# Seven products for the last two chunks in both layers, weight sums made in layer one's first half, token sums one step after the turned tile

## The chip, the cores and the metric

The kernel runs on one core of one Trainium2 chip. The time is the device time of one execution in microseconds (us), and what is compared is the median over several runs. Beside it there is one execution taken by the hardware profiler; its rows and spans are in us, with the mean of one instruction in ns. The engines are called as in the profile: PE (TensorE, the matrix products) with PEld (its weight loads), DVE (VectorE), ACT (ScalarE), POOL (GpSimd) and SP (SyncE, which mostly issues transfers, DMAs).

## The reference

The input x has 2048 tokens of 512 features. Four residual blocks follow each other: a linear attention, a gated mixer, and the same two again with the same weights. Everything is fp32.

```python
def _A_ref(x, wqkv, wo):                  # linear attention, 32 heads of 16
    q, k, v = ...                         # x @ wqkv, split by head
    phi = lambda t: jnp.where(t > 0, t + 1, jnp.exp(t)) + 1e-6
    pq, pk = phi(q), phi(k)
    kv = jnp.einsum("bhsd,bhse->bhde", pk, v)
    z = jnp.einsum("bhsd->bhd", pk)
    num = jnp.einsum("bhqd,bhde->bhqe", pq, kv)
    den = jnp.einsum("bhqd,bhd->bhq", pq, z)[..., None] + 1e-6
    return merged(num / den) @ wo

def _B_ref(x, w_in, w_sp, b_sp, w_out):   # w_in 512x1792, w_sp 2048x2048, w_out 896x512
    z = _gelu(jnp.einsum("bsd,df->bsf", x, w_in))
    z1 = z[..., :Fh]                      # Fh = 896
    z2 = _layernorm(z[..., Fh:], axis=-1)
    g = jnp.einsum("ts,bsf->btf", w_sp, z2) + b_sp[None, :, None]
    return jnp.einsum("bsf,fd->bsd", z1 * g, w_out)

x = x + _A_ref(_layernorm(x), A_wqkv, A_wo)
x = x + _B_ref(_layernorm(x), B_w_in, B_w_sp, B_b_sp, B_w_out)
x = x + _A_ref(_layernorm(x), A_wqkv, A_wo)
x = x + _B_ref(_layernorm(x), B_w_in, B_w_sp, B_b_sp, B_w_out)
```

## The kernel before

**Numbers.** Every fp32 operand is split into a high part, which ACT writes (`high`, L101), and a low part, the operand minus the high part, which DVE (`low`, L104) or POOL (L109) writes. A product of two operands is three products on PE into the same bank of PSUM: high by high, high by low, low by high (`mm3`, L115 to L117). PE is the engine that all others serve.

**Tiles and memory.** The 2048 tokens are 16 tiles of 128 rows; four tiles make a chunk of 512 tokens. Buffers come from pools that are written out by hand: `pages` (128x512, 22 of them, "pg" in the profile), `quads` (four times that, "qd"), `bigs` ("bg") and `banks` (the eight banks of PSUM). An instruction that takes a buffer waits until its last reader is done. Each engine executes its own instructions in the order of the program, so the order in the code is the order of the queues. A step issues work for several tiles at once: tile s at the start of the pipeline, tile s-1, s-2 and so on further down.

**A layer** (L = 0, "layer one", and L = 1, "layer two", the same code) is an attention and a mixer:

- *P1*, steps 1 to 17, the first half of the attention: normalise a tile (`ln_a`, `ln_b`), turn it (by PE against `ident` or by a trip through DRAM, L286), split it, project to keys and queries, sum the keys (on POOL, L372), and add the tile's product with its keys into four banks `G` (`Gmm`). For the very first tile `start` lets PE run idle products (L434) while operands are on their way.
- *transition*: the sum of the keys is scaled (L505), split with its low part on POOL, and multiplied by ones (L515, L516); `G` is split and multiplied down to the matrix `W2`. In between stand the score scalings of the first tiles (`a`, on POOL, L590; `a2_den` and `a2_mul`, on DVE).
- *P2*, steps 1 to 18: `b` splits a scaled query tile, `c` multiplies it by `W2`, `c2` adds the residual (L643), `c_stats` and `c3` normalise it and send it through DRAM to be turned, `d_high` and `d_low` (one step later) split the turned tile into its chunk's pair of quads `xT`, `e` makes the z2 half of the mixer's first product (448 columns at a time), `f` the z1 half (seven blocks of 128 features by four chunks, 12 products each). From step 8 on `sums.tick` makes sums of blocks of `w_sp` on POOL (L978), which both layers' *P4* need; in layer one P2 does so besides its own work.
- a tail of z1 products, then *P4*: the product with `w_sp`, made of seven products of half-size blocks in place of eight (L1103 to L1105), the gates (POOL, L1123 and L1125), and the product with `w_out` tile by tile (`o`, addition L1198, store L1200). While layer one's `o` runs, `join` begins the next layer's P1.

**Seven products for the last two chunks.** In layer two alone (`self.seven`), the z1 blocks 0 to 5 of the chunks 2 and 3 are not made by `f`. The features are paired (block g with block g + 3) and so are the chunks, and the 2x2 block product is made in seven products P1 to P7 in place of eight. This needs sums of blocks of the weight and sums of blocks of tokens. The weight sums are made in layer one's `o` loop by the class `Make` (load, four additions on DVE, split, store into the DRAM tile `kept`), and fetched in layer two's P2 by `fetch_sum` (POOL's queue). The token sums are made by DVE as each turned tile of chunk 3 arrives (`block_sums`, inside `d_low`), from that tile and the tile of chunk 2 that POOL has put together again (`whole`); `block_parts` splits them.

```python
            if s == 16:                       # part of side(), layer two's P2
                self.P2(1)
                self.P2(2)
                self.fetch_sum(2)
                for m in (2, 3):
                    self.block_parts(m, 0)
```

In layer one the same blocks are 12 products each of `f`, in the steps and in a loop ahead of P4.

Of the kernel before, what the change touches and what calls it, by code (L numbers as in the profile page):

```python
# [53 lines left out]
def mixer_kernel(ctx: ExitStack, tc: tile.TileContext, x_in, wqkv, wo_d, win1_d, win2_d, wsp_d, bsp_d, wout_d,  # L54
# [109 lines left out]

    class Make:


        def __init__(self):
            self.raw, self.sum, self.part = {}, {}, {}

        def fetch(self, g):
            self.raw[g] = load(win1_d[g]), load(win1_d[g + 3])

        def add(self, g):
            a, b = self.raw.pop(g)
            A11, A12, A21, A22 = (r.rearrange("p (c f) -> p c f", f=P)[:, s] for r in (a, b) for s in (slice(0, 2), slice(2, 4)))
            s, t = pages.get([P, 2, 2, P]), pages.get([P, 2, 2, P])
# [4 lines left out]
            pages.put(a, b)  # L182
            self.sum[g] = s, t

        def split(self, g):
            self.part[g] = []
            for r in self.sum.pop(g):
                h, l = pages.get([P, 2, 2, P], F32R), pages.get([P, 2, 2, P], F32R)
                split(h, l, r)
                pages.put(r)  # L190
                self.part[g] += [h, l]

        def store(self, g):
            for n, p in enumerate(self.part.pop(g)):
                m = 2 * (n // 2)
                nc.sync.dma_start(kept[:, m:m + 2, g, n % 2, :], p.bitcast(F32).rearrange("p m c f -> p m (c f)"))
                pages.put(p)

        def step(self, i):
            for g in range(3):  # L200
                at = i - 2 * g
                if 0 <= at < 5:
                    (self.fetch, lambda g: None, self.add, self.split, self.store)[at](g)
# [87 lines left out]
    class P1:  # L291
# [124 lines left out]
        def start(self):  # L416
# [19 lines left out]
            idle(10)  # L436
# [3 lines left out]
            self.wk.piece()  # L440
            self.T_high(0)
            idle(4)
# [3 lines left out]
            self.wk.piece()  # L446
# [9 lines left out]
        def run(self):  # L456
# [5 lines left out]
            for s in range(1, NT + 2):  # L462
# [34 lines left out]
                for w in list(side)[:1 if s < 5 else 2]:  # L497
                    w.fetch()

# [69 lines left out]
    class P2:  # L569
        def __init__(self, p1):  # L570
# [7 lines left out]
            self.seven = self.L == 1  # L578
            self.S, self.T, self.Tp = {}, {}, {}
# [92 lines left out]
        def d_low(self, i):  # L672
# [40 lines left out]
        def f(self):  # L713
# [8 lines left out]
            if f == NF - 1 and not (self.seven and n == 3):  # L722
                quads.put(*self.xT.pop(n))
# [15 lines left out]
        def whole(self, k):  # L739

            h, l = (t[:, :, k * P:(k + 1) * P].bitcast(F32) for t in self.xT[2])
            self.xr = pages.get([P, 4, P])
            nc.gpsimd.tensor_tensor(self.xr, h, l, op=OP.add)

        def block_sums(self, k, y):


            p, o = divmod(k, 2)
# [4 lines left out]
            x = self.xr  # L753
# [5 lines left out]
            pages.put(x)  # L759
# [42 lines left out]
        def P1(self, g):  # L802
            if g == 0:
                self.X, self.C = [], []
            self.X.append(banks.get(PAGE))
            self.product(self.X[g], "P1", g, start=True)
            self.C.append(self.copied(self.X[g]))

        def P2(self, g):
            y = banks.get(PAGE)  # L810
            self.product(y, "P2", g, start=True, stop=True)
            t = self.C[g]
# [4 lines left out]
        def last_f(self, n):  # L817
            self.fq.append((n, NF - 1))
            self.f()

        def tail(self, p4):
            self.last_f(3)
# [38 lines left out]
        def side(self, s):  # L861

            if s == 14:
                self.P1(0)
                self.P1(1)
            elif s == 15:
                self.P1(2)
                self.P2(0)
                self.fetch_sum(4)
            elif s == 16:  # L870
                self.P2(1)
                self.P2(2)
# [12 lines left out]
            if 13 <= s < 17:  # L885
                self.whole(s - 13)

        def run(self, sums):
            w1 = self.win1
            for s in range(1, NT + 3):  # L890
# [16 lines left out]
                else:  # L907
# [32 lines left out]
                if self.seven:  # L940
                    self.side(s)
# [59 lines left out]
    class P4:  # L1001
# [189 lines left out]
        def o(self, i):  # L1191
# [6 lines left out]
            nc.vector.tensor_add(x, x, b)  # L1198
            banks.put(b)
            nc.sync.dma_start(xs[2 * self.L + 2, i], x)  # L1200
# [117 lines left out]
```

## Time and profile before

| | before |
|---|---|
| median of 3 runs | 1393.01 us (1392.59 to 1393.34) |
| profiled execution: its own time | 1392.76 us |
| its span (first to last instruction) | 1391.0 us |
| granted clock of PE | 1.0 |
| PE busy | 1383.0 us, 99% of the span |
| DVE busy | 908.8 us, 65% |
| ACT busy | 595.1 us, 43% |
| POOL busy | 429.2 us, 31% |
| DMA traffic | 233.57 MB, mean 168 GB/s |

A row of the timeline or of a group gives the start (timeline only), the busy time, the engine, the line of the code, the operation, what it writes and reads, and the shapes. A bracket at the end of a timeline row is the idle time of that engine just before the instruction and what ended it. A row of a group ends with the number of instructions, their busy time, the mean of one in ns, and the idle time before them with what ended most of it. In the list of waits the three numbers are the sum, the count and the longest wait.

### The profile page before, as it was taken

How to read it: one execution, taken by the hardware profiler on the slowest of the kernel's cores; microseconds unless marked ns; L12 is line 12 of the kernel's file. 1: busy time of each engine (PE TensorE's matmuls, PEld its weight loads, DVE VectorE, ACT ScalarE, POOL GpSimd, SP SyncE). 2: the span in 40 equal slices, each digit the busy share in tenths (PEclk: the TensorE clock that was granted, in tenths of full speed). 3: DMA queues.
4: the chain of work that ended last, by engine and by line, in shares of the span. 5: the costliest groups of instructions: out<-in, count | busy, mean ns of one | idle time of the engine just before them, and what ended most of it. 6: DMA issues, size and time to landing. Idle time of an engine off the chain costs nothing.

```text
span 1391.0 us, 17707 instructions
## 1 busy us (share of the span) xinstructions
PE 1383.0 (99%) x6252; PEld 1159.9 (83%) x6252; DVE 908.8 (65%) x1305; ACT 595.1 (43%) x922; POOL 429.2 (31%) x518
## 2 busy tenths in 40 slices
PE   9999999999999999999999999999999999999998
PEld 7888888888888888888888888888878888888887
DVE  6785777853755587666667767876666345776642
ACT  6674543444442234241366755444454432342410
POOL 3343344544135541431023424432320001123310
PEclk9999999999999999999999999999999999999999
DMA  5541256766678864357745313555454323434442
GB/s 174 171 132 59 91 167 224 260 228 211 212 246 287 297 228 137 122 203 241 266 130 177 112 45 122 174 175 173 124 187 152 106 91 129 174 129 159 167 145 90
DMA packets 148313, 233.57 MB, mean 168 GB/s; under 512 B 12416, under 2 KB 54144, under 8 KB 148224
## 3 DMA queue, kind: packets, MB, share of 16 engines
q1 hardware_dynamic: 144768, 226.15, 49.0%
q0 software_dynamic: 1728, 3.15, 0.8%
q10 hardware_dynamic: 1728, 3.15, 0.6%
q8 instruction: 49, 0.80, 0.2%
q14 instruction: 40, 0.33, 0.1%
HBM read 161.35 MB, written 71.04 MB: 167 GB/s over the span
## 4 chain that ended last, share of the span: by engine, by line
PE 96%; DVE 2%; ACT 1%; POOL 1%; issue 1%; ACTq 0%; POOLq 0%
PE bank L117 18%; PE bank L116 18%; PE bank L115 18%; PE bank L1105 13%; PE bank L1104 13%; PE bank L1103 13%; PE bank L247 1%; PE bank L793 0%; PE bank L792 0%; PE bank L791 0%; DVE st L222 0%; PE bank L434 0%; ACT qd L101 0%; ACT pg L235 0%; DVE pg L286 0%
## 5 line engine op out<-in xcount | busy, mean ns | idle before, releaser
L1104 PE MATMUL bank<-qd,pg 128*128 128x512 f32 x800 | 311.2, 389 | 0.0
L1105 PE MATMUL bank<-qd,pg 128*128 128x512 f32 x800 | 311.2, 389 | 0.0
L1103 PE MATMUL bank<-qd,pg 128*128 128x512 f32 x800 | 311.2, 389 | 0.0
L1069 DVE TENSOR_TENSOR qd<-qd,qd 128x1024 fp32r<-128x1024 f32 x112 | 158.4, 1414 | 138.7 <-ACT qd L1062 138.5
L1062 ACT ACTIVATE qd<-qd 128x1024 fp32r<-128x1024 f32 x112 | 118.6, 1059 | 235.9 <-DMA qd<-s 96.5
L1125 POOL TENSOR_TENSOR bg<-bg,pg 128x512 f32<-128x512 f32 x56 | 78.2, 1399 | 327.6 <-DMA pg<-z 302.9
L1104 PEld LDWEIGHTS bank<-qd,pg 128*128 128x128 f32 x800 | 150.2, 188 | 31.4
L1103 PEld LDWEIGHTS bank<-qd,pg 128*128 128x128 f32 x800 | 150.2, 188 | 31.3
L1105 PEld LDWEIGHTS bank<-qd,pg 128*128 128x128 f32 x800 | 150.2, 188 | 30.8
L117 PE MATMUL bank<-qd,pg 128*128 128x512 f32 x384 | 149.9, 390 | 0.0
L226 POOL TENSOR_SCALAR rs<-mv 128x1 f32<-128x1 f32 x96 | 38.5, 401 | 333.5 <-DVE mv L224 320.3
L978 POOL TENSOR_TENSOR pg<-pg,pg 128x512 f32<-128x512 f32 x64 | 93.7, 1464 | 93.8 <-DMA pg<-in_wsp_dram 85.4
L235 ACT ACTIVATE pg<-pg,nb,rs 128x512 f32<-128x512 f32 x63 | 51.1, 811 | 161.8 <-POOL nb L229 155.6
L115 PE MATMUL bank<-qd,pg 128*128 128x512 f32 x288 | 112.3, 390 | 0.0
L116 PE MATMUL bank<-qd,pg 128*128 128x512 f32 x288 | 112.2, 390 | 0.0
L115 PE MATMUL bank<-bg,qd 128*128 128x448 f32 x256 | 94.2, 368 | 1.6 <-ACT qd L101 1.6
L117 PE MATMUL bank<-bg,qd 128*128 128x448 f32 x256 | 93.6, 366 | 0.1
L116 PE MATMUL bank<-bg,qd 128*128 128x448 f32 x256 | 93.6, 366 | 0.0
L101 ACT ACTIVATE pg<-pg 128x512 fp32r<-128x512 f32 (+1 forms) x83 | 51.0, 616 | 96.5 <-DVE pg L286 51.9
L115 PE MATMUL bank<-wo,qd 128*128 128x512 f32 x224 | 87.1, 389 | 0.0
L116 PE MATMUL bank<-wo,qd 128*128 128x512 f32 x224 | 87.1, 389 | 0.0
L117 PE MATMUL bank<-wo,qd 128*128 128x512 f32 x224 | 87.1, 389 | 0.0
(156 smaller groups left out, 2689.7 us busy)
## 6 DMA issues: line engine op xcount, KB each, us to landing
qd<-s SPq DMA_DIRECT2D x64, 512.0 KB, 3.4
qd<-in_wsp_dram SPq DMA_DIRECT2D x48, 512.0 KB, 4.2
pg<-in_wsp_dram SPq DMA_DIRECT2D x64, 256.0 KB, 5.0
s<-pg SPq DMA_DIRECT2D x64, 256.0 KB, 4.8
pg<-x SPq DMA_DIRECT2D x64, 256.0 KB, 3.3
pg<-z SPq DMA_DIRECT2D x56, 256.0 KB, 3.7
x<-pg SPq DMA_DIRECT2D x48, 256.0 KB, 2.6
z<-pg SPq DMA_DIRECT2D x44, 256.0 KB, 2.9
```

Source lines behind the costliest of these rows:

```text
L101: nc.scalar.activation(h, src, AF.Copy)
L115: nc.tensor.matmul(out, ah, bh, start=start, stop=False)
L116: nc.tensor.matmul(out, ah, bl, start=False, stop=False)
L117: nc.tensor.matmul(out, al, bh, start=False, stop=stop)
L235: nc.scalar.activation(y, x, AF.Identity, bias=nb, scale=rs)
L978: nc.gpsimd.tensor_tensor(t, a, b, op=OP.add)
L1062: nc.scalar.activation(w[:, 0], r, AF.Copy)
L1069: nc.vector.tensor_sub(w[:, 1], r, w[:, 0].bitcast(F32))
L1103: m(out, h[:, o], w[:, 0, j, :], start=start, stop=False, skip_group_check=True)
L1104: m(out, h[:, o], w[:, 1, j, :], start=False, stop=False, skip_group_check=True)
L1105: m(out, l[:, o], w[:, 0, j, :], start=False, stop=stop, skip_group_check=True)
L1125: nc.gpsimd.tensor_tensor(u, u, z1, op=OP.mult)
```

## The change

- The switch `self.seven` goes: both layers take the seven products for chunks 2 and 3, and both end P2 with `tail`.
- `Make` runs once, in layer one's P1 (steps 15 to 17) and P2 (steps 1 to 7), by the table `PLAN`: "f0" loads block pair 0, "a0" makes its four sums, "s0" splits one of the two result pages, and every step first stores what the step before split. The four sums are now made in place and on POOL, one depending on another; the order in `kept` follows (`FORMS`).
- The token sums stand one step later. `d_low` of chunk 3 keeps the turned tile in `held`, and `block_sums` (from step 15 on) takes it a step later, behind the next tile's `d_low`. It adds up the tile of chunk 2 on DVE, in place of `whole` on POOL. The splits `block_parts` move to the steps 17 (two of them) and 18 (six), the fetches of the weight sums to 16, 17 and 18; the forms P1 and P2 are spread over the steps 14 to 17.
- In the start, ten idle products become eight and four become two; the second piece of the key weight is split ahead of the first tile, in place of behind its high part.
- One more load for the sums of `w_sp` is issued at step 7 of P2; `nxt.T(1)` (split of the next layer's second tile) moves ahead of the last `o` of layer one; the last output tile of layer two is added and stored in two halves, the second half's store on ACT's queue.

The diff, cut to its core:

```diff
...
+    FORMS = (2, 4, 3, 1)
     class Make:
         def add(self, g):
-            nc.vector.tensor_add(s[:, 0], A21, A22)
-            nc.vector.tensor_sub(s[:, 1], s[:, 0], A11)
-            nc.vector.tensor_sub(t[:, 0], A11, A21)
-            nc.vector.tensor_sub(t[:, 1], A12, s[:, 1])
+            A11, A12, A21, A22 = (r[:, s] for r in self.raw[g] for s in (slice(0, 256), slice(256, 512)))
+            G = nc.gpsimd.tensor_tensor
+            G(A22, A21, A22, op=OP.add)
+            G(A21, A11, A21, op=OP.subtract)
+            G(A11, A22, A11, op=OP.subtract)
+            G(A12, A12, A11, op=OP.subtract)
         def split(self, g):
...
+            r = self.raw[g].pop(0)
+            h, l = pages.get(PAGE, F32R), pages.get(PAGE, F32R)
+            split(h, l, r)
+            pages.put(r)
+            self.part.append((g, 2 - 2 * len(self.raw[g]), h, l))
+        def store(self):
+            for g, m, *parts in self.part:
+                for n, p in enumerate(parts):
+                    nc.sync.dma_start(kept[:, m:m + 2, g, n, :], p.bitcast(F32).rearrange("p (m f) -> p m f", m=2))
+                    pages.put(p)
+            self.part = []
+        PLAN = {("P1", 15): ("f0",), ("P1", 16): ("a0", "f1"), ("P1", 17): ("s0", "a1"), ("P2", 1): ("s0",),
+                ("P2", 2): ("s1",), ("P2", 3): ("s1", "f2"), ("P2", 5): ("a2",), ("P2", 6): ("s2",), ("P2", 7): ("s2",)}
+        def step(self, at):
+            self.store()
+            for what in self.PLAN.get(at, ()):
+                {"f": self.fetch, "a": self.add, "s": self.split}[what[0]](int(what[1]))
...
-            idle(10)
+            idle(8)
             self.ln_a(0)
             self.ln_a(1)
             self.ln_b(0)
             self.wk.piece()
+            self.wk.piece()
             self.T_high(0)
-            idle(4)
+            idle(2)
             banks.put(b)
             pages.put(m, f)
             self.T_low(0)
-            self.wk.piece()
             self.ln_b(1)
             self.wk.piece()
             self.wk.piece()
...
                     side.popleft().piece()
                 for w in list(side)[:1 if s < 5 else 2]:
                     w.fetch()
+                if self.L == 0:
+                    make.step(("P1", s))
         def d_low(self, i):
             b, home, h, l = self.dpart
             low(l, b, h)
             n, k = divmod(i, 4)
-            if self.seven and n == 3:
-                self.block_sums(k, b)
-            home.put(b)
+            if n == 3:
+                self.held.append((k, b))
+            else:
+                home.put(b)
             if i in self.xB:
                 pages.put(self.xB.pop(i))
-            if k == 3 and not (self.seven and n >= 2):
+            if k == 3 and n < 2:
                 self.fnext = [(n, f) for f in range(NF)]
...
-        def whole(self, k):
+        def block_sums(self):
+            k, y = self.held.popleft()
+            x = pages.get([P, 4, P])
             h, l = (t[:, :, k * P:(k + 1) * P].bitcast(F32) for t in self.xT[2])
-            self.xr = pages.get([P, 4, P])
-            nc.gpsimd.tensor_tensor(self.xr, h, l, op=OP.add)
-        def block_sums(self, k, y):
+            nc.vector.tensor_add(x, h, l)
             p, o = divmod(k, 2)
             if o == 0:
                 for m in range(1, 5):
                     self.T[m, p] = pages.get([P, 2, 256])
             t = [None] + [self.T[m, p][:, :, o * P:(o + 1) * P] for m in range(1, 5)]
-            x = self.xr
             V = nc.vector
             V.tensor_sub(t[1], y[:, 0:2, :], x[:, 0:2, :])
             V.tensor_sub(t[2], y[:, 2:4, :], t[1])
             V.tensor_sub(t[3], y[:, 2:4, :], y[:, 0:2, :])
             V.tensor_sub(t[4], x[:, 2:4, :], t[2])
-            pages.put(x)
+            pages.put(x, y)
...
             self.S[m] = []
             for g in range(3):
                 t = pages.get([P, 2, 2, P], F32R)
-                nc.gpsimd.dma_start(t.rearrange("p i c f -> p i (c f)"), kept[:, m - 1, g])
+                nc.gpsimd.dma_start(t.rearrange("p i c f -> p i (c f)"), kept[:, FORMS.index(m), g])
...
         def side(self, s):
-            if s == 14:
-                self.P1(0)
-                self.P1(1)
-            elif s == 15:
-                self.P1(2)
-                self.P2(0)
+            if 15 <= s < 18:
+                self.P2(s - 15)
+            if 14 <= s < 17:
+                self.P1(s - 14)
+            if s == 16:
                 self.fetch_sum(4)
-            elif s == 16:
-                self.P2(1)
-                self.P2(2)
+            elif s == 17:
+                self.fq.append((2, NF - 1))
+                self.f()
+                self.block_parts(2, 0)
+                self.block_parts(3, 0)
                 self.fetch_sum(2)
-                for m in (2, 3):
-                    self.block_parts(m, 0)
-            elif s == 17:
-                self.last_f(2)
-                self.block_parts(2, 1)
-                self.block_parts(3, 1)
+            elif s == 18:
+                quads.put(*self.xT.pop(2))
+                for m, p in ((2, 1), (3, 1), (4, 0), (4, 1), (1, 0), (1, 1)):
+                    self.block_parts(m, p)
                 self.fetch_sum(3)
-            elif s == 18:
-                for m in (4, 1):
-                    for p in range(2):
-                        self.block_parts(m, p)
-            if 13 <= s < 17:
-                self.whole(s - 13)
...
                         self.d_low(s - 2)
+                if s >= 15:
+                    self.block_sums()
...
                 self.f()
                 self.f()
-                if self.seven:
-                    self.side(s)
+                self.side(s)
+                if self.L == 0:
+                    make.step(("P2", s))
                 self.fq.extend(self.fnext)
                 self.fnext = []
                 w1.piece(True)
                 w1.fetch()
+                if s == 7:
+                    sums.fetch()
                 if s > 7:
                     sums.tick()
-                if s >= NT + 1 and not self.seven:
-                    self.p4.fetch(s - NT - 1)
...
-            nc.vector.tensor_add(x, x, b)
+            out = xs[2 * self.L + 2, i]
+            if self.L == 1 and i == NT - 1:
+                for issue, s in ((nc.sync, slice(0, 256)), (nc.scalar, slice(256, 512))):
+                    nc.vector.tensor_add(x[:, s], x[:, s], b[:, s])
+                    issue.dma_start(out[:, s], x[:, s])
+            else:
+                nc.vector.tensor_add(x, x, b)
+                nc.sync.dma_start(out, x)
             banks.put(b)
-            nc.sync.dma_start(xs[2 * self.L + 2, i], x)
...
         def run(self, nxt):
             p2 = self.p2
-            if p2.seven:
-                p2.tail(self)
-            else:
-                self.prepare(0, 0)
-                self.fetch(2)
-                while p2.f():
-                    pass
-                p2.win1.free()
-                self.prepare(1, 1)
-                self.fetch(3)
-                self.prepare(None, 2)
+            p2.tail(self)
...
-            make = Make() if nxt is not None else None
             for i in range(NT):
                 self.loadx(i + 2)
                 self.gates()
+                if i == NT - 1 and nxt is not None:
+                    nxt.T(1)
                 self.o(i)
                 self.zsplit(i + 2)
-                if make is not None:
-                    make.step(i)
                 if nxt is not None:
                     self.join(i, nxt)
...
             if i == 14:
                 nxt.T(0)
-            if i == 15:
-                nxt.T(1)
     sums = Sums()
+    make = Make()
...
```

More of the change, by code (lines that the diff above doesn't have):

```diff
@@ L163, in mixer_kernel @@
     kept = dram.tile([P, 4, 3, 2, 256], F32, name="win1_sums")
+    FORMS = (2, 4, 3, 1)
     class Make:
         def __init__(self):
-            self.raw, self.sum, self.part = {}, {}, {}
+            self.raw, self.part = {}, []
         def fetch(self, g):
-            self.raw[g] = load(win1_d[g]), load(win1_d[g + 3])
+            self.raw[g] = [load(win1_d[g]), load(win1_d[g + 3])]
         def add(self, g):
-            a, b = self.raw.pop(g)
-            A11, A12, A21, A22 = (r.rearrange("p (c f) -> p c f", f=P)[:, s] for r in (a, b) for s in (slice(0, 2), slice(2, 4)))
@@ L193, in store @@
[L193 to L203, printed above, removed]
+            A11, A12, A21, A22 = (r[:, s] for r in self.raw[g] for s in (slice(0, 256), slice(256, 512)))
@@ L577, in __init__ @@
             self.fnext = []
-            self.seven = self.L == 1
-            self.S, self.T, self.Tp = {}, {}, {}
+            self.held = deque()
+            self.S, self.T, self.Tp, self.X = {}, {}, {}, {}
         def loadx(self, i):
@@ L721, in f @@
                 mm3(b, (w.h[:, f, c, :], w.l[:, f, c, :]), (h[:, c, :], l[:, c, :]), c == 0, c == 3)
-            if f == NF - 1 and not (self.seven and n == 3):
+            if f == NF - 1 and n < 2:
                 quads.put(*self.xT.pop(n))
```

23 lines of the change are left out of this document (5 added, 18 removed).

## The prediction

> **What bounds the kernel now.** I read the page's first part, then the waits of the tensor engine (PE), then windows of the timeline at the places that the change touches.
>
> ```profile
> span 1391.0 us, 17707 instructions
> PE 1383.0 (99%) x6252; PEld 1159.9 (83%) x6252; DVE 908.8 (65%) x1305; ACT 595.1 (43%) x922; POOL 429.2 (31%) x518
> PE bank L434 <- DVE pg L429: 2.3, 1, 2.3
> PE bank L115 <- ACT qd L101: 1.6, 1, 1.6
> ```
>
> PE is busy for 99% of the span and waits twice: at the start, and once for 1.6 us. Nothing else has to be hidden better; a change pays if it takes products away, takes PE's few waits away, or makes a new one. Any wait that another engine hands to PE is added to the end in full, because nothing later has slack to give it back.
>
> **The price of a product.** A busy time of 390 ns is not the price: products overlap.
>
> ```profile
> 990.41 0.39 PE L115 MATMUL bank<-qd,pg 128*128 128x512 f32 x1
> 992.90 0.39 PE L117 MATMUL bank<-qd,pg 128*128 128x512 f32 x1
> ```
>
> These are the first and the twelfth of one group: 2.49 us for 11 steps, 0.226 us each. A product of 448 columns takes 448/512 of that, 0.20.
>
> **1. Seven products in layer one.** Two chunks by six feature blocks took 12 products each, 144; seven forms by three blocks by six are 126. 18 x 0.226 = 4.07 us leave PE. The order of instructions of the two programs confirms it: 18 PE rows fewer (6161 against 6179). Gain 4.07.
>
> **2. The wait in layer two goes.** Step 16 puts the splits of two token sums in front of the turn of the last tile; the change puts them into steps 17 and 18.
>
> ```profile
> 1005.57 1.16 ACT L101 ACTIVATE qd<-pg 128x512 fp32r<-128x512 f32 x2 [0.40 <-ACT pg L733]
> 1006.23 2.22 DVE L104 TENSOR_TENSOR qd<-pg,qd 128x512 fp32r<-128x512 f32 x2 [2.17 <-ACT qd L101]
> 1008.13 0.39 PE L117 MATMUL bank<-qd,bg 128*128 128x512 f32 x1
> 1008.38 1.06 DVE L286 STREAM_TRANSPOSE pg<-pg 128x512 f32<-128x512 f32 x1
> 1009.48 0.63 ACT L101 ACTIVATE qd<-pg 128x512 fp32r<-128x512 f32 x1 [2.75 <-DVE pg L286]
> 1010.16 0.47 PE L115 MATMUL bank<-bg,qd 128*128 128x448 f32 x1 [1.64 <-ACT qd L101]
> 1011.19 0.36 PE L115 MATMUL bank<-bg,qd 128*128 128x448 f32 x1
> ```
>
> VectorE (DVE) works on the token sums until 1008.45, then turns tile 15; ScalarE splits it at 1009.48, and the tile's first product can only start at 1010.16. From 1008.13 to 1011.19 PE makes four steps, which should take 0.226 + 3 x 0.20 = 0.83: 2.23 us are lost. What is late next is the trip of the turned tile through DRAM:
>
> ```profile
> 308.95 0.69 DVE L643 TENSOR_TENSOR pg<-pg,bank 128x512 f32<-128x512 f32 x1 [4.77 <-PE bank L117]
> 317.92 1.10 DVE L286 STREAM_TRANSPOSE pg<-pg 128x512 f32<-128x512 f32 x1 [1.54 <-DMA pg<-yt]
> ```
>
> These are the same tile in layer one, where DVE does wait for it: 8.97 us from the residual add to the turn; with turn, split and low part (1.10 + 0.63 + 0.69) it is ready 11.4 us after the add. Until its products PE has 48 of 448 columns and 30 of 512, 16.4 us. So 5 us of slack; I take the whole 2.23 as gained, in a range of 1.8 to 2.23.
>
> **3. The layers' seam.** The second turned tile is now split ahead of the last output tile.
>
> ```profile
> 701.74 0.40 PE L116 MATMUL bank<-qd,pg 128*128 128x512 f32 x1
> 702.45 0.39 PE L115 MATMUL bank<-qd,pg 128*128 128x512 f32 x1
> ```
>
> Two steps took 0.71 instead of 0.45. Gain 0.25. The removed sums of weights stood beside a PE that was full there: nothing.
>
> **4. The start.** Four idle products fewer, and the second weight piece is split before the first tile.
>
> ```profile
> 2.32 4.45 PE L434 MATMUL bank<-pg,ones 128*128 128x512 f32 x10 [2.32 <-DVE pg L429]
> 7.95 0.44 PE L115 MATMUL bank<-qd,pg 128*128 128x512 f32 x1
> 11.39 0.40 PE L117 MATMUL bank<-qd,pg 128*128 128x512 f32 x1
> ```
>
> From the first to the twelfth real product 3.44 us pass, of which 11 steps need 2.49 and four transposes about 0.45. At most 0.5 can be gained; the lows of the later pieces still queue on DVE, so I take 0.3. The idle products themselves fill time in which operands are on their way, so dropping them gains nothing.
>
> **5. The end.** The last tile goes out in halves.
>
> ```profile
> 1387.09 0.69 DVE L1198 TENSOR_TENSOR pg<-pg,bank 128x512 f32<-128x512 f32 x1 [4.07 <-PE bank L117]
> 1387.80 0.33 SPq L1200 DMA_DIRECT2D out_dram<-pg  x1
> ```
>
> Two half adds take about 0.15 longer than one, but the second transfer, on ScalarE's queue, carries half and the first leaves 0.3 sooner. From 0.15 worse to 0.5 better; I take 0.2 better.
>
> **6. The sums of weights move in front of the transition of layer one.** This is where the change costs. GpSimd (POOL) gets eight dependent subtractions and additions of 256 columns (blocks 0 and 1) between its last sum of keys and the low part of that sum, which PE needs. ScalarE and DVE get a split ahead of the key sum's scaling and split, and that split waits for the first four.
>
> ```profile
> 121.99 1.29 POOL L372 TENSOR_TENSOR pg<-pg,pg 128x512 f32<-128x512 f32 x1 [4.25 <-DVE pg L367]
> 125.72 0.42 DVE L505 TENSOR_SCALAR pg<-pg 128x512 f32<-128x512 f32 x1
> 126.17 0.63 ACT L101 ACTIVATE pg<-pg 128x512 fp32r<-128x512 f32 x1 [1.09 <-DVE pg L505]
> 126.89 1.30 POOL L109 TENSOR_TENSOR pg<-pg,pg 128x512 fp32r<-128x512 f32 x1 [3.61 <-ACT pg L101]
> 129.30 0.40 PE L516 MATMUL bank<-pg,ones 128*128 128x512 f32 x1
> ```
>
> The last key sum ends at 123.28, the low part at 128.19, and its product runs at 129.30: POOL idles 3.61 us, and 1.1 us more are spare. Inputs are no limit: blocks 0 and 1 are loaded into pages that the Gram products of tiles 12 and 13 free, the later at 115.23 + 0.39:
>
> ```profile
> 115.23 0.39 PE L117 MATMUL bank<-pg,pg 128*128 128x512 f32 x1
> pg<-in_win_dram SPq DMA_DIRECT2D x34, 256.0 KB, 2.9
> ```
>
> so they have landed by about 118.6. No row shows POOL on 256 columns. The bounds and the gap between two dependent operations:
>
> ```profile
> L372 POOL TENSOR_TENSOR pg<-pg,pg 128x512 f32<-128x512 f32 x30 | 38.8, 1294 | 60.9 <-DVE pg L367 42.2 <-issue 13.9 <-PE bank L116 4.8
> L229 POOL TENSOR_SCALAR nb<-mv,rs 128x1 f32<-128x1 f32 x96 | 26.7, 279 | 9.5
> L1123 POOL TENSOR_TENSOR bg<-bg 128x512 f32<-128x512 f32 x12 | 23.6, 1964 | 57.5 <-DVE bg L1156 57.5
> 156.76 0.22 POOL L226 TENSOR_SCALAR rs<-mv 128x1 f32<-128x1 f32 x1 [0.94 <-DVE mv L224]
> 157.07 0.57 POOL L227 TENSOR_TENSOR rs<-rs,mhalf 128x1 f32<-128x1 f32 x1
> ```
>
> Halfway between 279 ns (one column) and 1294 (512) lies 0.79; the gap is 0.09. With p for one operation the low part ends at 123.28 + 8 (p + 0.09) + 1.30 = 125.3 + 8p, and PE stands still for S = 8p - 4.0: at 0.79, 2.3 us. The other branch (first four, split, scaling, high part) ends at 126.8 + 0.63 + 0.69 + 0.42 + 0.63 = 129.2, before POOL is through at 130.3. But DVE and POOL hold each other up when both read two tiles of SBUF:
>
> ```profile
> 165.64 1.29 POOL L590 TENSOR_TENSOR pg<-z_q,pg 128x512 f32<-128x512 f32 x1
> 166.17 1.31 DVE L611 SCALAR_TENSOR_TENSOR pg<-z_q,den 128x512 f32<-128x512 f32 x1
> ```
>
> (0.69 where POOL is idle.) The split's low part and the scaling may each push POOL back once, 0 to 1 us; I add 0.2. S = 2.5, range 1.2 to 3.3. Queued behind are the scores' scaling on POOL and the four Gram splits on ScalarE and DVE; they follow with PE's own delay. [...]
>
> **7. The rest of the splits** fall into the first steps of the second half. One stands ahead of a low part with little slack:
>
> ```profile
> 155.17 0.68 DVE L104 TENSOR_TENSOR pg<-bank,pg 128x512 fp32r<-128x512 f32 x1
> 156.30 0.39 PE L117 MATMUL bank<-qd,pg 128*128 128x512 f32 x1
> ```
>
> The low part ends 0.45 before its product; a split of 0.69 in front makes it 0.25 late. Cost 0.3, range 0 to 0.6. Block 2's sums (step 5) delay a normalisation by about 0.7, inside slack as in part 2. SP's queue gets six loads and twelve stores there, and is freed of them at the seam; none of the loads that follow is due within 3 us.
>
> **8. The tail of layer one** has what layer two's had and, besides, the sums of w_sp on POOL. VectorE's token sums (2.4 us a step) meet those additions, and the third fetch of sums waits on POOL behind the last tile's statistics:
>
> ```profile
> pg<-win_sums POOLq DMA_DIRECT2D x12, 256.0 KB, 4.1
> ```
>
> By my count of the queue it lands between 0.5 before and 1 us after its product is due. Cost 0.4, range 0 to 1.5.
>
> **Sum.** -4.07 - 2.23 - 0.25 - 0.3 - 0.2 + 2.5 + 0.3 + 0.4 = -3.85. The profiled execution took 1392.76 (span 1391.0), 0.25 under the median of 1393.01. So span 1387.2, and 1389.2 as a median.
>
> **Rivals.**
>
> *No new wait* (0.12): POOL needs 0.65 or less for 256 columns and the tail holds. For it: half of 1294 is 0.65. S = 1.2, parts 7 and 8 nothing: 1387.2.
>
> *Layer one's tail gives it back* (0.16). VectorE's additions wait for POOL's one after another, the splits for the sixth form or the fetch come 3 us late. For it: the 1.31 above; against: 5 us of slack at the turn. 1389.2 + 3 = 1392.2, no change that can be told.
>
> *Slower: POOL's price does not shrink with the columns* (0.07). The other terms sum to -6.35, so the change loses once S passes 6.35, p = 1.29, and by over 0.2% from p = 1.64. The subtraction inside one tile takes 1964 ns, and all eight write over one of their inputs too: S = 11.7, 1398.4. Against: 0.22 to 0.28 for one column.
>
> *A colder start* (0.07). [...]
>
> **Numbers.** My forecast 0.58. What a measurement of this kernel tells from no change is about 0.2%, 2.8 us: faster means under 1390.2. The forecast's own range (S 1.2 to 3.3, tail to 1.5) is 1387 to 1391.2, four fifths of it under 1390.2 (0.47); with no new wait (0.12), a third of the cold start and a part of the rest, faster 0.63. Slower by 0.2% is the third rival and a worse form of the second, 0.1. Same 0.27. The range takes in the second rival: 1386.5 to 1393.0.
>
> **What would show it.** In the profile after: PE's waits list a wait at the product of the key sum for POOL or DVE of 1.2 to 3.3 us near 129; POOL's 256-column row reads about 0.79; the wait at the last tile's products in layer two is gone; PE steps between products of layer one's last forms stay 0.23. I am wrong if the key sum's product starts without a gap, if POOL's row is over 1.2, or if layer one's tail shows gaps over 1.5 us.

## The result and the profile after

The changed kernel took 1406.8 us (1406.2 to 1408.0), the kernel before 1392.9 on the same chips: a ratio of 1.0101 (1.0083 to 1.0118), 13.9 us slower, where 3.85 us faster was forecast. The profiled execution took 1407.07 (span 1405.3) against 1392.76 (1391.0), 14.3 more. One execution among all of those below, of the kernel with both edits, fell into a slow state (1529.2 us at a mean granted clock of 0.851) and is left out of that kernel's figures.

The page of the changed kernel, and its list of PE's waits (sum, times, longest):

```profile
span 1405.3 us, 17790 instructions
PE 1389.5 (99%) x6230; PEld 1161.5 (83%) x6230; DVE 938.5 (67%) x1338; ACT 604.5 (43%) x939; POOL 442.8 (32%) x538
```

```profile
PE bank L115 <- ACT qd L101: 3.2, 2, 2.8
PE bank L436 <- DVE pg L431: 2.3, 1, 2.3
PE bank L793 <- ACT qd L101: 1.8, 1, 1.8
PE bank L520 <- POOL pg L109: 1.5, 1, 1.5
PE bank L794 <- DVE qd L104: 1.4, 1, 1.4
PE bank L115 <- ACT pg L101: 0.9, 1, 0.9
PE bank L117 <- DVE pg L104: 0.5, 1, 0.5
PE bank L793 <- DMA pg<-win_sums: 0.2, 1, 0.2
```

PE was to lose 18 products, 4.07 us, and it lost them (22 rows fewer, with four idle products of the start); its busy time grew by 6.5 all the same. The waits went from 3.9 us to 11.8, 7.9 more. With 4.07 us of products gone that should have made 3.8 us; 14.3 were measured, so products also took longer. The mean granted clock of the run fell from 1.0 to 0.994.

Landmarks on PE's timeline show the stage. First the kernel before, then the one after, at the same work: the first product of a group behind the transition (`bank<-bg,pg`), a tile in the second half (z2 half of tile 11), the first and the last P4 product of layer one, the first P4 product of layer two.

```profile
137.66 0.39 PE L115 MATMUL bank<-bg,pg 128*128 128x512 f32 x1
282.64 0.36 PE L115 MATMUL bank<-bg,qd 128*128 128x448 f32 x1
350.63 0.39 PE L1103 MATMUL bank<-qd,pg 128*128 128x512 f32 x1
621.95 0.39 PE L1103 MATMUL bank<-qd,pg 128*128 128x512 f32 x1
1038.69 0.39 PE L1103 MATMUL bank<-qd,pg 128*128 128x512 f32 x1
```

```profile
146.34 0.39 PE L115 MATMUL bank<-bg,pg 128*128 128x512 f32 x1
294.40 0.36 PE L115 MATMUL bank<-bg,qd 128*128 128x448 f32 x1
367.92 0.39 PE L1096 MATMUL bank<-qd,pg 128*128 128x512 f32 x1
639.29 0.39 PE L1096 MATMUL bank<-qd,pg 128*128 128x512 f32 x1
1053.31 0.39 PE L1096 MATMUL bank<-qd,pg 128*128 128x512 f32 x1
```

The delay is 8.68 us behind the transition (0.4 of it was there before the key sum's product), 11.76 at tile 11, 17.29 where P4 begins, 17.34 where its last group ends, and 14.62 at layer two's P4. So the loss is all in layer one ahead of P4, in three places: the transition 8.7, the steps of the second half 3.1, the tail 5.5, which is 9.6 when the 4.07 for the products that went is added back. The seam and layer two gained 2.7 up to there, and 0.3 more by the end.

**The transition.** The additions on POOL, the scaling of the key sum on DVE (L509, 0.42 in the kernel before), and the product that waits, in the changed kernel:

```profile
127.25 1.21 POOL L181 TENSOR_TENSOR pg<-pg,pg 128x256 f32<-128x256 f32 x1
128.54 0.80 POOL L182 TENSOR_TENSOR pg<-pg,pg 128x256 f32<-128x256 f32 x1
129.42 0.73 POOL L183 TENSOR_TENSOR pg<-pg 128x256 f32<-128x256 f32 x1
130.12 1.27 POOL L109 TENSOR_TENSOR pg<-pg,pg 128x512 fp32r<-128x512 f32 x1
```

```profile
127.78 0.97 DVE L509 TENSOR_SCALAR pg<-pg 128x512 f32<-128x512 f32 x1
```

```profile
129.47 0.51 PE L519 MATMUL bank<-pg,ones 128*128 128x512 f32 x1
131.44 0.50 PE L520 MATMUL bank<-pg,ones 128*128 128x512 f32 x1 [1.47 <-POOL pg L109]
```

An addition takes 0.74 (the first here, which meets DVE, 1.21), the low part ends at 131.39, and its product comes 1.97 us after the first one where 0.23 is the step in the kernel before (129.07 to 129.30): 1.74 us, by the chain that the prediction has. The other 6.5 us stand in the windows (busy time of each engine, then the granted clock in the column behind POOL), of the kernel before and of the changed one:

```profile
129.00:132.00 3.00, 3.00 (x26) 2.86 (x26) 1.29 (x3) 1.72 (x3) 1.59 (x2) 1.00 0.34 87
132.00:137.00 5.00, 5.00 (x37) 4.61 (x37) 4.81 (x14) 0.87 (x3) 3.41 (x3) 1.00 0.01 3
```

```profile
129.00:132.00 3.00, 1.43 (x7) 0.71 (x6) 2.07 (x4) 2.39 (x6) 2.31 (x3) 1.00 0.12 45
132.00:146.00 14.00, 14.00 (x58) 13.03 (x58) 6.89 (x17) 3.15 (x6) 4.18 (x3) 0.51 0.01 2
```

Right behind the wait, from 132.3 to 145.9, the clock is halved. PE counts as fully busy there, and no list of waits shows it, but most of the 48 small products that follow and of the twelve large ones behind them run at half speed: 0.21 us a small product, where 0.11 is the step in the kernel before. Half of 13.65 us is 6.8, about what is to be explained.

**The tail of layer one.** Four views of the changed kernel: POOL, ACT, PE, and DVE's low parts grouped from 331 to 351.

```profile
319.14 2.67 POOL L971 TENSOR_TENSOR pg<-pg,pg 128x512 f32<-128x512 f32 x2
321.90 0.22 POOL L228 TENSOR_SCALAR rs<-mv 128x1 f32<-128x1 f32 x1
```

```profile
323.17 0.81 ACT L237 ACTIVATE pg<-pg,nb,rs 128x512 f32<-128x512 f32 x1 [3.16 <-POOL nb L231]
323.89 0.61 ACT L101 ACTIVATE qd<-pg 128x512 fp32r<-128x512 f32 x1
```

```profile
347.66 0.49 PE L793 MATMUL bank<-qd,pg 128*128 128x512 f32 x1 [1.75 <-ACT qd L101]
349.53 0.50 PE L794 MATMUL bank<-qd,pg 128*128 128x512 f32 x1 [1.37 <-DVE qd L104]
```

```profile
L104 DVE TENSOR_TENSOR qd<-pg,qd 128x512 fp32r<-128x512 f32 x7 | 8.8, 1299 | 3.5 <-ACT qd L101 3.5
```

The statistics that POOL gets at 319.94 stand behind two sums of w_sp until 321.90; ACT's normalisation waits for them, and behind it in ACT's queue stands the split of another tile (tile 14), whose turn was done at 320.92. PE waits for that split from 321.8 to 324.56. Then DVE is late: its low parts take 1.30 on average where 0.69 is usual, since POOL's sums run at the same time, the token sums follow, and PE waits twice more, 3.5 us together by the starts of the products. From 350.7 the clock is halved once more, for 3.4 us.

**Layer two's tail** has no wait left; the last tile's first product follows at once:

```profile
1025.07 0.39 PE L117 MATMUL bank<-qd,bg 128*128 128x512 f32 x1
1025.30 0.36 PE L115 MATMUL bank<-bg,qd 128*128 128x448 f32 x1
```

### The profile page after: what moved, and what is told of

It is laid out like the page before. It is cut to its first block, busy times and chain, and to the rows that moved or that the text cites. A ratio compares the mean times of both kernels' runs of the same rounds, so it can differ in the third digit from the quotient of the medians.

```text
span 1405.3 us, 17790 instructions
## 1 busy us (share of the span) xinstructions
PE 1389.5 (99%) x6230; PEld 1161.5 (83%) x6230; DVE 938.5 (67%) x1338; ACT 604.5 (43%) x939; POOL 442.8 (32%) x538
## 4 chain that ended last, share of the span: by engine, by line
PE 74%; DVE 2%; ACT 1%; POOL 1%; issue 1%; DMA 0%; ACTq 0%; DVEq 0%; POOLq 0%
PE bank L1096 13%; PE bank L1098 13%; PE bank L1097 13%; PE bank L117 11%; PE bank L116 11%; PE bank L115 11%; PE bank L793 1%; PE bank L794 1%; PE bank L795 1%; DVE qd L104 1%; DVE st L224 0%; DMA pg<-win_sums 0%; PE bank L249 0%; DVE pg L750 0%; POOL rs L229 0%
## 5 line engine op out<-in xcount | busy, mean ns | idle before, releaser
L1118 POOL TENSOR_TENSOR bg<-bg,pg 128x512 f32<-128x512 f32 x56 | 78.3, 1398 | 321.8 <-DMA pg<-z 312.0
L1098 PEld LDWEIGHTS bank<-qd,pg 128*128 128x128 f32 x800 | 150.2, 188 | 31.4
L1097 PEld LDWEIGHTS bank<-qd,pg 128*128 128x128 f32 x800 | 150.2, 188 | 31.1
L1096 PEld LDWEIGHTS bank<-qd,pg 128*128 128x128 f32 x800 | 150.2, 188 | 31.0
L117 PEld LDWEIGHTS bank<-qd,pg 128*128 128x128 f32 x384 | 72.5, 189 | 17.2 <-DVE pg L104 2.0
```

The lines of the kernel that those rows point to most:

```text
L117: nc.tensor.matmul(out, al, bh, start=False, stop=stop)
L1096: m(out, h[:, o], w[:, 0, j, :], start=start, stop=False, skip_group_check=True)
L1097: m(out, h[:, o], w[:, 1, j, :], start=False, stop=False, skip_group_check=True)
L1098: m(out, l[:, o], w[:, 0, j, :], start=False, stop=stop, skip_group_check=True)
L1118: nc.gpsimd.tensor_tensor(u, u, z1, op=OP.mult)
```

## The experiments

All times are medians beside the kernel before on the same chip (1392.8 to 1393.5).

**Is it the wait or the clock?**

```diff
+        if p2.L == 0:
+            for _ in range(6):
+                nc.tensor.matmul(zb, ones, zh, start=True, stop=True)
         nc.tensor.matmul(zb, ones, zh, start=True, stop=False)
         nc.tensor.matmul(zb, ones, zl, start=False, stop=True)
```

> The changed kernel, in which layer one's transition repeats the product of the key sum's high part with ones six times ahead of the one that counts (same bank, each starts the sum afresh). They fill the 1.47 us in which PE waits for the low part. Clock theory: what costs most at the transition is not the wait but the clock, which was granted at 0.50 from 132.3 to 145.9; with PE busy in the wait it stays at 1.0, the 48 small products and the 12 large ones behind them take 0.11 and 0.23 again, and the kernel gains 6.8 us: 1400.0. Rival (the clock falls with the wait for data itself, or with the small products): the half clock stays, the six products are hidden, 1406.8.

Measured 1399.15 (1398.5 to 1400.4), 7.65 less than the changed kernel. The low part comes no sooner; the clock behind it is whole:

```profile
129.00:132.00 3.00, 2.77 (x13) 1.74 (x11) 2.09 (x4) 2.35 (x6) 2.32 (x3) 1.00 0.03 12
132.00:137.00 5.00, 5.00 (x48) 5.00 (x46) 3.52 (x10) 1.86 (x4) 2.52 (x2) 1.00 0.02 3
```

Six products that nobody needs save 7.65 us. In the profiled execution the same product behind the transition (146.34 in the changed kernel) comes at 139.88, 6.5 us sooner. That execution was 8.4 us faster in all; most of the rest (1.8) came from the tail, where the clock held too this time. So the clock was the larger part of the transition's price, and with PE at work in the wait it held (1.00 from 129 to 137).

**Is it the place or the engine?** In the next kernel the additions stand where they stood, on VectorE.

```diff
-            G = nc.gpsimd.tensor_tensor
+            G = nc.vector.tensor_tensor
```

> The changed kernel with the four sums of each block pair on VectorE in place of POOL, at the same places. [...] Theory A (POOL's price is the cause): no wait, clock 1.0, 8.6 us gained, 1398.2, and less where POOL delayed the statistics in step 5. Theory B (the place is the cause): four additions of 0.42 and a split of 0.69 stand ahead of the scaling of the key sum on VectorE, the low part comes some 2.4 us later than in the kernel before where 1.1 were spare, so a wait of 1.3 to 1.8 us remains and the clock falls again: 1405 to 1407.

Measured 1399.15 (1398.6 to 1399.5).

```profile
130.88 0.50 PE L520 MATMUL bank<-pg,ones 128*128 128x512 f32 x1 [0.85 <-POOL pg L109]
```

```profile
132.00:137.00 5.00, 4.95 (x44) 4.81 (x43) 3.62 (x10) 1.55 (x4) 2.53 (x2) 1.00 0.01 3
```

Theory B is right that a wait remains, though at 0.85 it is under the 1.3 to 1.8 of its estimate, and theory A is nearer on the time. Neither had the reason: the wait only shrank, from 1.47 to 0.85, and in this execution the clock held behind it. The last section shows that the length alone does not decide that. A wait is left because VectorE's additions and the split stand ahead of the scaling there, which starts at 128.40 where it was 125.72 in the kernel before.

**The sums moved behind the transition.**

```diff
+        PLAN = {("P2", 1): ("f0",), ("P2", 3): ("a0",), ("P2", 4): ("s0",), ("P2", 5): ("s0", "f1"), ("P2", 7): ("a1",),
+                ("P2", 8): ("s1",), ("P2", 9): ("s1", "f2"), ("P2", 11): ("a2",), ("P2", 12): ("s2",), ("P2", 13): ("s2",)}
```

> The changed kernel with the table of the weight sums moved behind the transition: loads in steps 1, 5 and 9 of the second half, additions (still on POOL) in 3, 7 and 11, splits in 4-5, 8-9 and 12-13. Theory (POOL's eight additions ahead of the key sum's low part make the wait, the wait halves the clock): the product of the key sum's low part follows the high part's with no wait, clock 1.0, and the transition gives back 8.6 us: about 1398.2, with up to 2 on either side for what the sums cost in their new steps. Rival (the key sum is late for another reason, such as the earlier splits of the weight pieces): the wait near 130 stays, 1406 to 1407.

Measured 1411.75 (1411.2 to 1412.8), a miss of 13.5. The wait at the key sum is gone and the clock there is 1.0, as the theory says, but the same additions now stand ahead of statistics for a normalisation:

```profile
PE bank L115 <- ACT qd L101: 8.6, 5, 2.9
PE bank L249 <- ACT pg L237: 2.5, 1, 2.5
```

Between 175 and 306 PE loses 0.3 to 2.7 us at seven places, and behind two of them the clock is halved for 3.4 us. The middle of the second half, which had lost 3.1 in the changed kernel, has no room for these sums: it lost 12.2 us here. The tail lost 3.8 us more than in the changed kernel, with the clock halved twice in it, and why was not followed.

**The tail without sums of w_sp.**

```diff
-                if s > 7:
+                if 7 < s < 15:
                     sums.tick()
...
-                if g in (1, 4, 7) or 8 <= g < 28:
+                if g < 28:
                     self.sums.tick()
```

> The changed kernel without the sums of w_sp in steps 15 to 18 of layer one's second half; the four ticks are made up in the first steps of layer one's P4. Theory (POOL's w_sp sums hold up the statistics and VectorE's token sums): the gap of 3.15 us at 321 falls under 0.6, the two at 345 to 350 (2.14 and 1.87) go with the 3.4 us at half clock behind them, 6 to 8 us in all: 1399 to 1401. Rival (VectorE's own token sums and splits are what is late): the gap at 321 shrinks by at most 1.3, those at 345 to 350 stay, 1405 to 1406.

Measured 1400.48 (1399.6 to 1401.4), 6.3 less. In its tail:

```profile
L104 DVE TENSOR_TENSOR qd<-pg,qd 128x512 fp32r<-128x512 f32 x8 | 4.9, 680 | 2.2 <-ACT qd L101 2.2
```

```profile
322.23 0.47 PE L115 MATMUL bank<-bg,qd 128*128 128x448 f32 x1 [0.92 <-ACT qd L101]
```

The low parts take 0.68 again, the wait at the turned tile falls from 2.8 to 0.92, and no half clock follows. POOL's sums were the cause of the greater part; 1 us at the turned tile and 1 us ahead of the last forms remain. Layer one's P4, where the ticks were made up, takes 1.3 us longer than in the kernel before. That holds for all five kernels with this edit: 0.5 to 3.0 us in their profiles, with waits of PE for ACT or DVE there, against at most 0.5 in the five others that take seven products in layer one.

**Both edits.** The splits and token sums are as in the change.

> The changed kernel with the two edits that each gained alone: the sums of the weight blocks on VectorE, and no sums of w_sp in steps 15 to 18 of layer one. Alone they gained 7.65 and 6.3 us. Theory (two separate places, the transition and the tail, each with its own wait and its own stretch at half clock): the gains add, 1406.8 - 7.65 - 6.3 = 1392.9, within 1 us. Rival (the later splits and token sums on VectorE, which now also carries the weight sums, or a wait that the first gain uncovers): at least 2 us less, 1395 or more.

Measured 1394.5 (median of nine), between theory and rival. The profiled execution shows one reason that the gains do not add: layer one's P4 lost 2.9 us, 1.6 more than with the second edit alone. Six of its runs were granted a mean clock of 1.0 and took 1391.3 to 1394.8; three were granted 0.996 and took 1397.9 to 1400.3. A mean of 0.996 over 1393 us is some 11 us at half clock, near the stretch of 13.65 that the transition had in the changed kernel: with a wait of 0.85 us at the key sum, the clock of one program seems to hold in some runs and to fall in others. Where it fell in those three was not seen.

**Without the making of the sums.** Twelve transfers put raw blocks in their place. The products are the same in number and shape, but the kernel leaves the sums out and computes something else; only its time counts.

```diff
+        def copy(self, g):
+            for m in (0, 2):
+                for n in range(2):
+                    nc.sync.dma_start(kept[:, m:m + 2, g, n, :], win1_d[g + 3 * (m // 2)].rearrange("p (m f) -> p m f", m=2))
+        PLAN = {("P1", 8): 0, ("P1", 10): 1, ("P1", 12): 2}
```

> The changed kernel without the making of the weight sums: in their place twelve transfers from DRAM to DRAM put the raw blocks where the sums would be (steps 8, 10 and 12 of layer one's first half), so that no engine adds or splits; seven products run in both layers on these values. Theory (the sums' making costs 8.6 us at the transition and 2.9 in the second half's steps): 1406.8 - 11.5 = 1395.3, no wait at the key sum, the clock at 1.0 there, and the tail of layer one as late as before. Rival (seven products in layer one cost it by themselves in these places): 1400 or more.

Measured 1394.8 (1393.7 to 1397.0), 12.0 less: the sums' making costs what the landmarks say of the transition and the middle (8.7 + 3.1). In its profile these landmarks come 0.5 and 0.8 us later than in the kernel before, where they came 8.7 and 11.8 later in the changed one.

> As the last kernel (raw blocks in place of the weight sums, no engine makes them), and no sums of w_sp in steps 15 to 18 of layer one. Theory (with both costs away the product count and layer two give what the prediction summed): 1395.3 - 6.3 = 1389.0, against 1389.2 forecast for the change. Rival (VectorE's token sums in layer one's tail cost over 2 us without POOL's additions too): 1391 to 1393.

Measured 1389.05 (1387.1 to 1392.3). The edit of the ticks is added here. With both costs away it is faster than the kernel before by 3.9 us (ratio 0.9971, 0.9962 to 0.9980). Parts 1 to 5 of the prediction sum to 7.05 without the sums, so some 3 us are still lost; its profile, of a run at the lower end (1387.25), shows under 1 us of waits behind the start, and where the rest goes in the slower runs stays open. That 1389.05 is near the 1389.2 forecast for the whole change is chance: the forecast had 3.2 us of costs in it that this kernel does not have.

**Another place for the sums.** Blocks one after another in the first half, ahead of the key sum, beside the edit of the ticks.

```diff
+        PLAN = {('P1', 7): ('f0',), ('P1', 8): ('a0',), ('P1', 9): ('s0',), ('P1', 10): ('s0', 'f1'), ('P1', 11): ('a1',), ('P1', 12): ('s1',), ('P1', 13): ('s1', 'f2'), ('P1', 14): ('a2',), ('P1', 15): ('s2',), ('P1', 16): ('s2',)}
```

> The changed kernel with the weight sums made earlier in layer one's first half, block by block (loads in steps 7, 10, 13, additions on POOL in 8, 11, 14, splits in 9-10, 12-13, 15-16), so that they are done before the key sum, and no sums of w_sp in steps 15 to 18 of layer one. Theory (the sums cost because of where they stand; in the first half POOL is busy for a third of the time and PE waits for nothing): between the kernel without the making of the sums, 1389.05, and 1 us more: 1389 to 1390, below the kernel before. Rival (no place in layer one is free: VectorE and ScalarE are busy for 80 to 90% there, and each split or addition of POOL that VectorE meets is handed to PE): 1391 to 1394.

Measured 1397.0 (1394.7 to 1398.7): the rival, and worse than it, though VectorE and ScalarE are busy for 71 to 80% of that stretch in the kernel before (60 to 100 us), not for 80 to 90.

```profile
PE bank L115 <- ACT z_h L101: 3.4, 4, 2.1
```

PE now waits for the splits of turned tiles in the first half, once with 3.4 us at half clock behind it. By the landmarks the key sum's product comes 8.0 us later than in the kernel before, and P4, with the ticks made up there, loses 3.0.

> As the last kernel, with every step of the table two steps later (loads in 9, 12 and 15, additions in 10, 13 and 16, the last two splits in step 17 and in step 1 of the second half), where VectorE has more room, but one addition stands two steps and one split one step ahead of the key sum. Theory (only the eight additions right ahead of the key sum cost, since four leave the spare 1.1 us): 1389 to 1390.5, the key sum without a wait. Rival (one block's additions and a split ahead of the key sum are enough for a wait of 0.5 us or more, and beside the small products that may be enough for the clock to fall): 1391 to 1398.

The same table two steps later: 1400.0 (1399.3 to 1404.5). One block's additions and a split ahead of the key sum left a wait of 0.85 us there. In the profiled run the clock was halved at the small products again; but that run is the slowest of the four (1404.5, clock 0.995, the others 1399.3 to 1400.1 at 0.998 or 0.999), so the others did without most of it. The first half had waits of 2.4 and 1.7 us besides. No place tried in layer one was free.

**Seven products in layer two alone.** The switch `self.seven` and the old output loop with `Make` are back; the later token sums, the split ahead of the last output tile, the start and the halved last tile stay.

> Seven products in layer two alone, as in the kernel before, with the weight sums in layer one's output loop as before; kept from the change: the later token sums in layer two, the split ahead of layer one's last output tile, the shorter start, the halved last tile. Theory (parts 2, 3 and 5 of the prediction were right; layer two with the seam took 2.7 us less in the changed kernel, the end 0.3): 1393.1 - 2.7 - 0.3 = 1390.1, the start within 0.5 of nothing. Rival (layer two was faster only because something in layer one was moved out of it): 1392 to 1393.

Measured 1390.2 (1389.8 to 1390.7), ratio 0.9978 (0.9969 to 0.9988): faster than both kernels, by 2.7 and 16.6 us. PE's list of waits has one line left:

```profile
PE bank L436 <- DVE pg L431: 2.3, 1, 2.3
```

**The start.** Ten and four idle products and the old order of the weight piece, in that version:

> Seven products in layer two alone (the version that took 1390.2), with the start of the kernel before: ten and four idle products, the second piece of the key weight split behind the first tile's high part. Theory (part 4 of the prediction was wrong in sign: in the traces the first Gram product comes at 20.26 in the kernel before and between 20.15 and 20.87, 20.41 in the middle, in the nine kernels with the shorter start): 0.1 to 0.2 us better than the same kernel with the shorter start, so 1390.0 to 1390.1. Rival (the shorter start is worth the 0.3 us that the prediction took): 1390.5.

> Seven products in layer two alone with the shorter start, unchanged, as the partner of the kernel with the old start on the same chip: 1390.2, and below the kernel before by 2.7 us, within 0.5.

Measured 1390.39 (old start) and 1390.38 (shorter start): the start is worth nothing that can be told.

## Why the prediction was wrong

Parts 1, 2, 3 and 5 hold. Layer two with the seam gained 2.7 against 2.48 summed (0.27 up to layer two's first tile, where 0.25 was forecast, and 2.3 from its tile 11 to P4, where it was 2.23), the wait at the last tile is gone and nothing is late in its place; the version with seven products in layer two alone, which has the parts 2, 3, 4 and 5, gained 2.7 where these sum to 2.98 with part 4 and 2.68 without. Part 4 took 0.3 and got nothing.

Part 6 failed in its price, not in its wait. The chain was sized rightly: 0.74 to 0.80 for an addition against 0.79 taken, one collision with DVE as allowed for, 1.74 us of wait in a range of 1.2 to 3.3. The step that failed is the sentence of the first part that a wait "is added to the end in full": here a wait is added more than in full, 1.74 us of it and 6.5 of half clock behind it. PE's speed was taken up in one rival alone, the colder start, and not at the transition, where 60 products stand behind the wait. No run shows that start or a price of it: the old and the shorter start took 1390.39 and 1390.38 us.

Part 7 found one price rightly (0.3 for the low part at step 2; its step was 0.43 and the one behind it 0.34) and called the rest slack. That slack was none: a normalisation that is late holds up, in ACT's queue, the split of another tile. The same place in the kernel before and, at the step of block 2, in the changed kernel:

```profile
194.85 0.82 ACT L235 ACTIVATE pg<-pg,nb,rs 128x512 f32<-128x512 f32 x1 [5.12 <-POOL nb L229]
206.06 0.82 ACT L237 ACTIVATE pg<-pg,nb,rs 128x512 f32<-128x512 f32 x1 [6.11 <-POOL nb L231]
```

ACT idles until POOL's statistics come, with the split that PE needs right behind; it did so before, but now for 1.0 us more, and PE loses 0.6 at that tile. The middle lost 3.1 in such pieces of 0.2 to 0.7, against 0.3. The other pieces were not followed one by one; that the sums' making is behind them is shown by the kernel without it.

Part 8 was sized at 0.4 and cost 9.6. It had the meeting of DVE and POOL, but for the turned tile it relied on part 2's "5 us of slack". That sum has 11.4 us from the residual add to the low part, with the split right behind the turn, and counts PE's products of layer two. In the changed layer one it took 16.3 us for tile 14 (add at 308.97, low part done at 325.23): the turn came 1.9 us later than summed, and 3.0 us passed between its end and the split, a wait that the sum puts at nothing. Statistics, normalisation and split form one chain through three queues, and POOL's sums of w_sp stand in it. The second rival had the tail at 3 us. The gaps over 1.5 us in layer one's tail are the sign of being wrong that the prediction named. The half clock made the tail's cost more, and so, as I read it, did the steps themselves: with the products of the form f taken out, the distance from tile 12's z2 products to tile 13's is 10.3 us where it was 13.1, and POOL, ACT and DVE have the same work to do in it.

The range ended at 1393.0, because its worst case was one cost at a time. The changed kernel had three, and two of them with the clock.

## What to carry to other kernels

A wait of PE is not priced by its length. Before work is put ahead of one of PE's operands, look at the clock behind the wait as well: here, with 48 small products behind it, a wait of 1.47 us had 13.65 us at half clock after it, and one of 0.85 us had a halved clock after it in one profiled execution of three. A few repeated products in the wait may be a cheap cure: six saved 7.65 us here. Where an engine's queue mixes chains of several tiles, slack is what the whole queue has, not what one tile has; and slack counted with one layer's products does not hold in another, where the steps are shorter and POOL has other work. Work that is moved out of one place may have to be paid in the next: the five kernels that make up the ticks in P4 lost 0.5 to 3.0 us there.

## What the runs showed of the hardware

In windows of the changed kernel (the granted clock is the third number from the end):

```profile
132.00:133.00 1.00, 1.00 (x8) 1.00 (x7) 0.41 (x1) 1.00 (x2) 0.35 (x1) 0.63 0.00 0
145.00:146.00 1.00, 1.00 (x4) 0.81 (x3) 0.09 (x1) 0.00 (x0) 0.00 (x0) 0.54 0.00 0
351.00:354.00 3.00, 3.00 (x9) 2.32 (x8) 1.49 (x3) 2.03 (x4) 3.00 (x5) 0.50 0.61 199
```

By the trace's record of the clock it was halved from 132.26 to 145.91, 13.65 us, and from 350.71 to 354.13, 3.41 us. In the first of these stretches the small products (128 columns) follow each other in 0.21 us and the large ones (512) in 0.43, against 0.11 and 0.23 at the same place in the kernel before.

The length of a wait does not tell whether the clock falls. Behind the longest in the changed kernel, 2.8 us at 321, it stayed at 1.00 (324 to 345); behind the 1.47 us at the key sum it was halved from 132.26 on. The wait of 0.85 us at the key sum stands in three profiled executions: with the additions on VectorE the clock was 1.00 from 132 to 137, with both edits its mean over the run was 1.0, and with the sums two steps later it was halved at the small products. With six repeated products in the 1.47 us it was 1.00 from 129 to 137. What decides it, no run shows.
